# Pinning the order of the gates' products and the pd additions on VectorE, in a spectral filter with a feed-forward block

## Chip, cores and metric

The kernel runs on one core of a Trainium2 chip. The metric is the device time of one execution in microseconds (us); before the change its median is 2563.24 us over 3 runs (2560.34 to 2566.03). TensorE is called PE here, with PEld for its weight loads; VectorE is DVE, ScalarE is ACT, GpSimd is POOL, and SP issues the DMAs.

## What is computed

The input has 8 batches of 3008 rows with 256 columns. The first half filters each batch in the frequency domain; the second is a feed-forward block with a gate:

```python
X = np.fft.rfft(x, axis=1)
Yr = Xr @ w_r - Xi @ w_i + b_r
Yi = Xr @ w_i + Xi @ w_r + b_i
Y  = soft_threshold(Yr, 0.01) + 1j * soft_threshold(Yi, 0.01)
y  = np.fft.irfft(Y, n=3008, axis=1)
h  = y @ w_in
g  = h * np.clip(h + 3.0, 0.0, 6.0) / 6.0
out = g @ w_out
```

w_in has 256 x 2048 elements, w_out 2048 x 256. The change touches the feed-forward block alone, and there the gate, g.

## The kernel before

**Tiles and units.** The 24064 rows are cut into 47 chunks of 512 (T). The 2048 hidden columns are cut into 8 pairs of 128. A unit is one chunk with one such pair, so there are 376 units, numbered i in the order of `units` (line 595). A unit computes h of 2 x 128 hidden columns by 512 rows, its gate, and its share of the chunk's output. Operands of large products are split into a rounded part and the rest (hi and lo), and a product is three matmuls: lo x hi, hi x lo, hi x hi.

**The product with w_in.** It is a Strassen-like scheme with seven blocks of three matmuls (`block`, line 598) in four phases. Phase a (line 612) puts block 2 into PSUM bank pd and block 1 into bank pb; ACT copies pb out as p1 (`kept`, line 602), and DVE adds pd and p1 into the first quarter of h (`added`, line 607). Phase b adds block 6 to pb and copies it out as u2. Phase c adds block 7 to pb, puts block 5 into bank pc, copies pb out as u3, and DVE adds pc and u3 into another quarter of h. Phase d adds block 4 to pb and block 3 to pc; ACT copies pb into h (line 639), and DVE adds pc and u2 into the last quarter. pd and pc have one bank each, pb has two; the transforms' ps_a has two, and the output's po0 and po1 have one each.

**The gate** (`gate`, line 642) is a generator of two steps. The first lets ACT compute r = relu(h + 3) (line 646). The second lets DVE make the product min(r, 6) * h (line 648, a SCALAR_TENSOR_TENSOR over 128 x 1024 elements), and then splits it: ACT casts it to the rounded half of gs (line 131), DVE subtracts that to get the rest (line 132). There are 3 buffers of h, 2 of r and 2 of gs.

**The product with w_out** (`down`, line 660) has 24 matmuls per unit in four steps (line 671). The first 16 read the rounded half of gs, the last 8 the rest.

**The order of the work.** The loop at line 758 traces iteration i in this order: phase a of unit i, second step of the gate of unit i-2, then in turns a quarter of `down` of unit i-3, phase c of unit i-1, phase b of unit i, and phase d of unit i-1 followed by the first step of its gate. After each quarter `fill` (line 746) hands out pieces of other work: the transforms of later batches, the preparation of later chunks and, at the start, the decoding of weights. This traced order is not the order in which the engines run it. The tile framework plans the whole program with a simulated timeline: on each engine it takes, from what is ready in the plan, what was traced first or was marked with `tc.high_priority()`. The additions (line 610) and the copies out of PSUM (line 605) are marked so; the product of the gate is not. On the chip each engine then runs its queue in the order that was planned, and waits on semaphores where operands or buffers are not ready. `tc.issue_after(ins)` adds an edge to the plan: what is traced within it on the engine of `ins` is queued behind `ins`, without a wait for its end.

Of the kernel before, what the change touches and what calls it, by code (L numbers as in the profile page):

```python
# [2 lines left out]

# [1 line left out]

# [10 lines left out]
ALU = mybir.AluOpType  # L16
# [85 lines left out]
def spectral_ffn(ctx: ExitStack, tc: tile.TileContext, x, w_r, w_i, bias, w_in, w_out, f47, f64, g64, sgn, out):  # L102
    nc = tc.nc
# [11 lines left out]
    def space(shape, dt, name, tag=None):  # L115
        tag = tag or name
        return sb.tile(shape, dt, name=name, tag=tag, bufs=depth.get(tag, 1))
# [11 lines left out]
    def split(hi, lo, src, on=None):  # L129

        nc.scalar.copy(out=hi, in_=src)  # L131
        (on or nc.vector).tensor_tensor(out=lo, in0=src, in1=hi.bitcast(F32), op=ALU.subtract)  # L132
# [29 lines left out]
    def loaded(src, rows, cols, name, at=None):  # L162

        hi = const.tile([rows, cols], F32R, name=name + "_hi")
        lo = const.tile([rows, cols], F32R, name=name + "_lo")
        st = const.tile([rows, cols], F32, name=name + "_all") if at is None else at
        nc.sync.dma_start(out=st[:rows, :cols], in_=src)
        return hi, lo, st[:rows, :cols]
# [200 lines left out]
    with tc.issue_after(stores[-1].ins):  # L369
        r, k = [loaded(w, P, 2 * D, n, t) for w, n, t in ((w_r, "w_r", spare[7]), (w_i, "w_i", spare[8]))]  # L370
# [222 lines left out]
            yield  # L593

    units = [(c, f) for c in range(NC) for f in range(nf)]
    hs, ps_of, keep, gs, pos = {}, {}, {}, {}, {}

    def block(i, n, ps, start):
        c, f = units[i]
        product(ps, [(tuple(t[:, f, WEIGHT[n]] for t in win_s), yb[c, n])], start=start, more=True)  # L600

    def kept(i, n, ps):
        t = keep[i, n] = space([P, H], F32, n)
        with tc.high_priority():
            nc.scalar.copy(out=t, in_=ps)  # L605

    def added(i, u, half, ps, n):
        to = hs[i][:, u, half * H : (half + 1) * H]
        with tc.high_priority():
            nc.vector.tensor_tensor(out=to, in0=ps, in1=keep.pop((i, n)), op=ALU.add)  # L610

    def phase_a(i):
        pb = ps_b.tile([P, 512], F32, name="pb")[:, :H]
        pd = ps_c.tile([P, 512], F32, name="pd")[:, :H]
        ps_of[i] = pb
        hs[i] = space([P, 2, T], F32, "h")
        block(i, 2, pd, True)
        block(i, 1, pb, True)
        kept(i, "p1", pb)
        added(i, 0, 0, pd, "p1")  # L620

    def phase_b(i):
        block(i, 6, ps_of[i], False)
# [2 lines left out]
    def phase_c(i):  # L626
        pc = ps_c.tile([P, 512], F32, name="pc")[:, :H]
        block(i, 7, ps_of[i], False)
        block(i, 5, pc, True)
        kept(i, "u3", ps_of[i])  # L630
        added(i, 1, 1, pc, "u3")
        keep[i, "pc"] = pc

    def phase_d(i):
        pb, pc = ps_of.pop(i), keep.pop((i, "pc"))
        block(i, 4, pb, False)
        block(i, 3, pc, False)
        with tc.high_priority():
            nc.scalar.copy(out=hs[i][:, 1, :H], in_=pb)  # L639
        added(i, 0, 1, pc, "u2")  # L640

    def gate(i):

        h = hs.pop(i)
        r = space([P, 2, T], F32, "r")
        nc.scalar.activation(out=r, in_=h, func=AF.Relu, bias=three, scale=1.0)  # L646
        yield
        nc.vector.scalar_tensor_tensor(out=r, in0=r, scalar=6.0, in1=h, op0=ALU.min, op1=ALU.mult)  # L648
        t = gs[i] = space([P, 2, 2, T], F32R, "gs")
        split(t[:, 0], t[:, 1], r)  # L650
        yield
# [105 lines left out]
    n = len(units)  # L757
    for i in range(n + 3):
        for kind, f in ((in_band, i), (out_band, i - 3)):
            while 0 <= f < nf and (kind, f) not in ready:  # L760
                turn(LATE)
        if i < n:
            phase_a(i)
        gated(i - 2)
        fill(4 * i)
        if 0 <= i - 3 < n:
            down(i - 3, 0)
        if 0 <= i - 1 < n:
            phase_c(i - 1)
        fill(4 * i + 1)  # L770
        if 0 <= i - 3 < n:
            down(i - 3, 1)
        if i < n:
            phase_b(i)
        fill(4 * i + 2)
        if 0 <= i - 3 < n:
            down(i - 3, 2)
        if 0 <= i - 1 < n:
            phase_d(i - 1)
            gates[i - 1] = gate(i - 1)  # L780
            gated(i - 1)
        fill(4 * i + 3)
        if 0 <= i - 3 < n:
            down(i - 3, 3)
            gs.pop(i - 3)
# [47 lines left out]
```

## Time and profile before

| what | value |
|---|---|
| median of 3 runs | 2563.24 us (2560.34 to 2566.03) |
| the profiled execution | 2567.17 us |
| its span, first to last instruction | 2565.4 us |
| granted TensorE clock, mean of the span | 0.989 |
| PE busy | 2502.4 us (98%), 20910 matmuls |
| PEld busy | 2442.0 us (95%) |
| DVE busy | 1964.3 us (77%), 3189 instructions |
| ACT busy | 1821.1 us (71%), 3584 instructions |
| POOL busy | 773.4 us (30%) |
| chain that ended last, by engine | PE 88%, DVE 5%, DMA 3%, ACT 3% |

The profiled execution is one run; its own time is 3.9 us above the median, and its span 1.8 us below its time. Busy time is that of an engine's instructions, with overlaps counted once; matmuls are pipelined, so that the duration of one is longer than the distance to the next. A wait in the list of waits is idle time of an engine that ended when another engine, or a DMA, released it. Idle time of an engine that is not the bottleneck costs nothing by itself.

### The profile page before, as it was taken

To read this page: it belongs to the slowest core of one execution; us is meant where nothing else is said; L and a number is where in the kernel's file an instruction comes from. 1 tells how busy PE (TensorE), PEld (TensorE's weight loads), DVE (VectorE), ACT (ScalarE), POOL (GpSimd) and SP (SyncE) were. 2 spreads that over 40 slices of the span, in tenths; PEclk is the share of its full clock that TensorE was granted. 3 is DMA by queue.
4 is the path that set the end of the run, shared out by engine and by line. 5 is a ranking of instruction groups with operands and counts; after the bars stand their busy time and mean duration, and the time that the engine had idled before them with its cause. 6 is when DMAs were issued, how large, how long until landed. Compare 5 with 4: busy or idle time off the path is not lost.

```text
span 2565.4 us, 53388 instructions
## 1 busy us (share of the span) xinstructions
PE 2502.4 (98%) x20910; PEld 2442.0 (95%) x20910; DVE 1964.3 (77%) x3189; ACT 1821.1 (71%) x3584; POOL 773.4 (30%) x738
## 2 busy tenths in 40 slices
PE   5889999999999999999999999999999999999999
PEld 4579999999999999999999999999999999999998
DVE  7778878878787777777777777877777778676766
ACT  5477777777767777777777777767777777776766
POOL 3343342333222332323323333233321221121310
PEclk8889999999999999999999999999999999999999
DMA  8633432332222322323223222222221121110000
GB/s 241 196 112 108 125 103 81 93 91 68 60 71 85 91 68 61 94 72 95 69 71 92 68 79 76 83 77 83 68 78 57 55 66 51 37 33 25 13 18 17
DMA packets 150115, 200.54 MB, mean 78 GB/s; under 512 B 16847, under 2 KB 103943, under 8 KB 149863
## 3 DMA queue, kind: packets, MB, share of 16 engines
q1 hardware_dynamic: 149863, 197.13, 26.4%
q8 instruction: 164, 2.69, 0.4%
q14 instruction: 88, 0.72, 0.1%
HBM read 97.45 MB, written 74.97 MB: 67 GB/s over the span
## 4 chain that ended last, share of the span: by engine, by line
PE 88%; DVE 5%; DMA 3%; ACT 3%; issue 1%; POOL 0%; SPq 0%; ACTq 0%; DVEq 0%; POOLq 0%
PE po L671 38%; PE pb L160 18%; PE pc L160 9%; PE ps_a L140 7%; PE ps_a L160 7%; PE pd L160 5%; PE ps_a L137 3%; ACT r L646 1%; ACT gs L131 1%; DVE r L648 1%; DMA scr<-a 1%; DVE gs L132 1%; DMA zt<-tc 1%; DMA st<-in_w_out 0%; DMA st<-in_w_in 0%
## 5 line engine op out<-in xcount | busy, mean ns | idle before, releaser
L671 PE MATMUL po<-gs,w_out_hi 128*128 128x256 f32 x6016 | 1026.2, 277 | 0.0
L671 PEld LDWEIGHTS po<-gs,w_out_hi 128*128 128x128 f32 x6016 | 840.9, 188 | 1.6
L648 DVE SCALAR_TENSOR_TENSOR r<-r,h 128x1024 f32<-128x1024 f32 x376 | 481.1, 1280 | 273.0 <-ACT r L646 272.0
L671 PE MATMUL po<-gs,w_out_lo 128*128 128x256 f32 x3008 | 597.1, 278 | 3.5 <-ACT gs L131 2.7
L646 ACT ACTIVATE r<-h,three 128x1024 f32<-128x1024 f32 x376 | 434.5, 1155 | 214.9 <-DVE h L610 212.4
L160 PE MATMUL pb<-yb,w_in_hi 128*128 128x256 f32 x3008 | 565.2, 277 | 1.1 <-DVE yb L132 1.1
L132 DVE TENSOR_TENSOR gs<-r,gs 128x1024 fp32r<-128x1024 f32 x376 | 484.4, 1288 | 100.8 <-ACT gs L131 97.1
L131 ACT CAST gs<-r 128x1024 fp32r<-128x1024 f32 x376 | 395.4, 1052 | 107.5 <-DVE r L648 104.1
L671 PEld LDWEIGHTS po<-gs,w_out_lo 128*128 128x128 f32 x3008 | 457.6, 188 | 8.2 <-ACT gs L131 6.8
L160 PEld LDWEIGHTS pb<-yb,w_in_hi 128*128 128x128 f32 x3008 | 456.9, 188 | 4.7 <-DVE yb L132 1.3
L160 PE MATMUL pb<-yb,w_in_lo 128*128 128x256 f32 x1504 | 425.0, 285 | 2.7 <-ACT yb L131 1.7
L132 POOL TENSOR_TENSOR yb<-T,yb 128x256 fp32r<-128x256 f32 x184 | 171.7, 936 | 821.4 <-ACT yb L131 786.1
L610 DVE TENSOR_TENSOR h<-pc,u 128x256 f32<-128x256 f32 x752 | 314.4, 418 | 113.3 <-PE pc L160 100.8
L605 ACT COPY u<-pb 128x256 f32<-128x256 f32 x752 | 279.3, 373 | 86.5 <-PE pb L160 75.0
L160 PE MATMUL pc<-yb,w_in_hi 128*128 128x256 f32 x1504 | 295.0, 277 | 1.1 <-DVE yb L132 1.1
L160 PEld LDWEIGHTS pb<-yb,w_in_lo 128*128 128x128 f32 x1504 | 283.1, 189 | 8.6 <-ACT yb L131 1.9
L160 PEld LDWEIGHTS pc<-yb,w_in_hi 128*128 128x128 f32 x1504 | 228.2, 189 | 2.2 <-DVE yb L132 1.3
L160 PE MATMUL pc<-yb,w_in_lo 128*128 128x256 f32 x752 | 213.3, 284 | 0.7 <-DVE h L610 0.5
L605 ACT COPY p<-pb 128x256 f32<-128x256 f32 x376 | 139.5, 371 | 61.9 <-PE pb L160 59.9
L639 ACT COPY h<-pb 128x256 f32<-128x256 f32 x376 | 141.5, 376 | 48.6 <-PE pb L160 47.4
L610 DVE TENSOR_TENSOR h<-pd,p 128x256 f32<-128x256 f32 x376 | 156.7, 417 | 12.3 <-ACT p L605 11.5
L132 POOL TENSOR_TENSOR xs<-xin,xs 120x512 fp32r<-120x512 f32 (+1 forms) x45 | 58.4, 1297 | 340.9 <-ACT xs L131 320.6
(147 smaller groups left out, 4006.4 us busy)
## 6 DMA issues: line engine op xcount, KB each, us to landing
bt<-scr SPq DMA_DIRECT2D x96, 256.0 KB, 3.0
scr<-pt SPq DMA_DIRECT2D x96, 256.0 KB, 2.4
zt<-tc SPq DMA_DIRECT2D x376, 64.0 KB, 2.0
out<-ot SPq DMA_DIRECT2D x94, 256.0 KB, 2.1
scr<-a SPq DMA_DIRECT2D x96, 240.0 KB, 2.7
qt<-scr SPq DMA_DIRECT2D x96, 240.0 KB, 3.4
xin<-in_x SPq DMA_DIRECT2D x42, 480.0 KB, 4.5
f<-in_f SPq DMA_DIRECT2D x96, 128.0 KB, 2.8
```

The source lines that it names most:

```text
L131: nc.scalar.copy(out=hi, in_=src)
L132: (on or nc.vector).tensor_tensor(out=lo, in0=src, in1=hi.bitcast(F32), op=ALU.subtract)
L137: first = first()
L140: m()
L160: nc.tensor.matmul(**m)
L605: nc.scalar.copy(out=t, in_=ps)
L610: nc.vector.tensor_tensor(out=to, in0=ps, in1=keep.pop((i, n)), op=ALU.add)
L639: nc.scalar.copy(out=hs[i][:, 1, :H], in_=pb)
L646: nc.scalar.activation(out=r, in_=h, func=AF.Relu, bias=three, scale=1.0)
L648: nc.vector.scalar_tensor_tensor(out=r, in0=r, scalar=6.0, in1=h, op0=ALU.min, op1=ALU.mult)
L671: nc.tensor.matmul(out=pos[dh][:, cols], lhsT=w[:, ft * D + dh * P : ft * D + (dh + 1) * P], rhs=g[:, low, u, cols], start=f == 0 and u == ...
```

## The change

The additions into the first quarter of h are kept by unit in `sums`. When the second step of the gate of unit i is traced, the addition of unit i+2 has just been traced, in phase a of the same iteration. The product is now traced within `tc.issue_after` of that addition, so that DVE's queue has it behind the pd addition of unit i+2. The gates of units 374 and 375, for which there is no such addition, are as before. The cast and the subtraction of the gate get no edge of their own.

```diff
-from contextlib import ExitStack
+from contextlib import ExitStack, nullcontext
...
     units = [(c, f) for c in range(NC) for f in range(nf)]
+    sums = {}
...
     def added(i, u, half, ps, n):
         to = hs[i][:, u, half * H : (half + 1) * H]
         with tc.high_priority():
-            nc.vector.tensor_tensor(out=to, in0=ps, in1=keep.pop((i, n)), op=ALU.add)
+            return nc.vector.tensor_tensor(out=to, in0=ps, in1=keep.pop((i, n)), op=ALU.add)
...
         kept(i, "p1", pb)
-        added(i, 0, 0, pd, "p1")
+        sums[i] = added(i, 0, 0, pd, "p1")
...
         yield
-        nc.vector.scalar_tensor_tensor(out=r, in0=r, scalar=6.0, in1=h, op0=ALU.min, op1=ALU.mult)
+        with tc.issue_after(sums[i + 2].ins) if i + 2 in sums else nullcontext():
+            nc.vector.scalar_tensor_tensor(out=r, in0=r, scalar=6.0, in1=h, op0=ALU.min, op1=ALU.mult)
```

## Rows read from the trace of the kernel before

**Rows 1.** Busy us of each engine by stretch (xinstructions), then clock, DMA.
```profile
200.00:2290.00 2090.00, 2083.39 (x17733) 2056.87 (x17733) 1629.05 (x2653) 1515.25 (x2999) 637.87 (x600) 1.00 0.26 76
2290.00:2545.00 255.00, 254.18 (x2203) 252.11 (x2202) 177.60 (x273) 178.79 (x340) 55.03 (x59) 1.00 0.05 18
...
sum 2566.00, PE 2502.36 PEld 2442.04 DVE 1964.30 ACT 1821.10 POOL 773.44; mean PE 625.59 PEld 610.51 DVE 491.07 ACT 455.27 POOL 193.36
```

**Rows 2.** Waits of the whole run: who waited for whom, us, times, longest.
```profile
DVE r L648 <- ACT r L646: 272.0, 291, 2.5
ACT r L646 <- DVE h L610: 212.4, 240, 2.7
```

**Rows 3.** Waits of PE, then of PEld, from 200 us to the end.
```profile
PE po L671 <- ACT gs L131: 2.7, 4, 1.3
...
PE pd L160 <- DVE h L610: 1.0, 2, 0.7
...
PEld po L671 <- ACT gs L131: 6.6, 16, 1.6
PEld pd L160 <- DVE h L610: 2.1, 5, 0.9
...
PEld pc L160 <- DVE h L610: 1.4, 5, 0.5
```

**Rows 4.** DVE's timeline at three places: start, duration, what, idle time before.
```profile
159.33 1.22 DVE L648 SCALAR_TENSOR_TENSOR r<-r,h 128x1024 f32<-128x1024 f32 x1
...
161.93 0.42 DVE L610 TENSOR_TENSOR h<-pd,p 128x256 f32<-128x256 f32 x1
...
1509.44 0.41 DVE L610 TENSOR_TENSOR h<-pd,p 128x256 f32<-128x256 f32 x1
1509.84 1.23 DVE L648 SCALAR_TENSOR_TENSOR r<-r,h 128x1024 f32<-128x1024 f32 x1
...
2546.60 1.23 DVE L648 SCALAR_TENSOR_TENSOR r<-r,h 128x1024 f32<-128x1024 f32 x1 [1.28 <-ACT r L646]
2547.75 0.42 DVE L610 TENSOR_TENSOR h<-pd,p 128x256 f32<-128x256 f32 x1
```

**Rows 5.** Groups of the page: count, busy us, mean ns, idle before, releaser.
```profile
L648 DVE SCALAR_TENSOR_TENSOR r<-r,h 128x1024 f32<-128x1024 f32 x376 | 481.1, 1280 | 273.0 <-ACT r L646 272.0
...
L646 ACT ACTIVATE r<-h,three 128x1024 f32<-128x1024 f32 x376 | 434.5, 1155 | 214.9 <-DVE h L610 212.4
...
L610 DVE TENSOR_TENSOR h<-pd,p 128x256 f32<-128x256 f32 x376 | 156.7, 417 | 12.3 <-ACT p L605 11.5
```

**Rows 6.** Timeline of one unit's gate in the last stretch.
```profile
2332.74 1.23 DVE L648 SCALAR_TENSOR_TENSOR r<-r,h 128x1024 f32<-128x1024 f32 x1 [1.28 <-ACT r L646]
2332.86 0.38 ACT L605 COPY p<-pb 128x256 f32<-128x256 f32 x1
...
2333.99 1.05 ACT L131 CAST gs<-r 128x1024 fp32r<-128x1024 f32 x1 [0.45 <-DVE r L648]
...
2335.11 0.30 PEld L671 LDWEIGHTS po<-gs,w_out_lo 128*128 128x128 f32 x2
```

**Rows 7.** Timeline of one unit's gate in the middle stretch.
```profile
1540.69 1.22 DVE L648 SCALAR_TENSOR_TENSOR r<-r,h 128x1024 f32<-128x1024 f32 x1
1540.80 0.39 ACT L605 COPY p<-pb 128x256 f32<-128x256 f32 x1
...
1541.95 1.05 ACT L131 CAST gs<-r 128x1024 fp32r<-128x1024 f32 x1 [0.45 <-DVE r L648]
...
1544.43 0.30 PEld L671 LDWEIGHTS po<-gs,w_out_lo 128*128 128x128 f32 x2
```

**Rows 8.** Line 648 alone in the last stretch: length, DVE busy (xinstructions).
```profile
2290.00:2545.00 255.00, 59.25 (x48) 1.00 0.05 18
```

**Rows 9.** Sums over five stretches with the addition first, and five with the product first.
```profile
sum 232.00, PE 231.06 PEld 228.81 DVE 185.26 ACT 170.32 POOL 68.65; mean PE 46.21 PEld 45.76 DVE 37.05 ACT 34.06 POOL 13.73
...
sum 754.00, PE 751.36 PEld 742.97 DVE 571.36 ACT 538.77 POOL 223.86; mean PE 150.27 PEld 148.59 DVE 114.27 ACT 107.75 POOL 44.77
```

## The prediction

> **What bounds the kernel now.** I read the busy time of each engine by stretches first, since a share over the whole run averages over stages. In all, TensorE (PE) is busy for 2502.36 us of the 2565.4 us span and VectorE (DVE) for 1964.30 us. Before 200 us the kernel warms up and the gates hardly run; from 200 to 2290 us, where the transforms of later batches run beside the feed-forward units, PE is busy for 2083.39 of 2090 us; from 2290 to 2545 us, where little but the units is left, for 254.18 of 255 us [rows 1]. DVE has room in both: 1629.05 of 2090 us and 177.60 of 255 us. So PE is the bound, and an order on DVE matters only by what it makes PE wait for.
>
> Then the waits. DVE stands idle for 272.0 us before products (line 648) until ScalarE (ACT) has made the relu, and ACT for 212.4 us before relus until DVE has made the additions [rows 2]. Both look large, and both are idle time of engines that are not the bound. What counts is PE's own list, from 200 us on: its weight loads and matmuls wait 6.6 + 2.7 = 9.3 us for a gate's cast (ACT, line 131), 2.1 + 1.0 = 3.1 us for additions before they may write bank pd, and 1.4 us for additions before bank pc [rows 3]. These are 13.8 us, 0.5% of the run, and all that this change can take from PE's waits on gates and additions; PE's work itself is untouched.
>
> **What the change does to the queue.** It adds and removes no operation and no transfer, and neither SP's nor GpSimd's queue is passed. It pins an order: the product of unit i is issued on DVE behind the pd addition of unit i+2. In 101 of the 374 pairs the trace has this order already, as at 1509.44 and 1509.84 us; in 273, from the product at 159.33 us (its addition at 161.93) to that at 2546.60 us (its addition at 2547.75), the product comes first [rows 4]. The last two gates have no such addition and stay free. The edge is one of issue order, so no semaphore is added; but the addition needs its own operand, the p copy of ACT (line 605), so that in practice the product now waits for that too, and the subtraction behind the product, the later additions to h and the other DVE work wait with it. The planner lays out all queues anew around the edge, so PE's and ACT's orders move as well.
>
> **Part 1, the addition that goes ahead.** It was held by at most one product of 1.28 us [rows 5]. PE pays for that only where pd is reused at once: 3.1 us in all [rows 3]. Below nothing it can't go by itself, as an addition issued earlier frees the bank earlier. Bounds: 0 and -3.1 us. I take the share of pairs that change, 273/374 x 3.1 = -2.3 us.
>
> **Part 2, the product that comes later.** Its path is relu, product, cast, and then the first weight load of po, which opens the unit's last product on PE. Two units show both ends. At 2332.74 us the product starts as soon as the relu is there; the p copy ends at 2332.86 + 0.38 = 2333.24, and with 0.42 us for the addition the product could start at 2333.66: 0.92 us late. Now its cast ends at 2333.99 + 1.05 = 2335.04 and PE's load comes at 2335.11, so only 0.07 us of cover stand against it, and 0.85 us would be left on PE [rows 6]. At 1540.69 us the delay is 1540.80 + 0.39 + 0.42 - 1540.69 = 0.92 us again, but the cast ends at 1541.95 + 1.05 = 1543.00 and PE's load comes at 1544.43: 1.43 us of cover, nothing left [rows 7]. The cover is PE's other queued work; without it each of the 273 would cost up to 0.92 us.
>
> Bounds: 0, where the cover holds or the planner, which now knows of the later cast, lays other matmuls in between; and 48 products in the last stretch [rows 8] x 0.85 = +41 us, if each were like the one at 2332.74 and PE's order stayed. I take neither end. What is left of waits in a planned order is where the chip runs later than the plan; the present cast waits of 9.3 us are that. The path grows from 1.155 + 1.28 + 1.05 = 3.49 us to 4.41 us, by 26%; with as many misses per us of path, 9.3 x 0.26 = +2.4 us [rows 3, 5, 6]. This is an estimate.
>
> **Part 3, what comes next.** With the product later, an addition to h from pc that is ready can pass ahead of it or of the subtraction behind the cast, and so the next relu can start earlier: that is the 212.4 us of [rows 2], and against the 0.92 us of delay it is a gain of the same size. I cost it at nothing, between -1.4 us (the waits for bank pc, [rows 3]) and 0.
>
> **The sum:** -2.3 + 2.4 + 0 = +0.1 us. A second reading supports it. The kernel holds both orders in long stretches. In five where all 35 products already follow their addition (581 to 614, 690 to 732, 979 to 1023, 1475 to 1522 and 1961 to 2027 us) PE is busy for 231.06 of 232 us, 99.60%; in five where 116 of 119 precede it (341 to 539, 1529 to 1577, 1602 to 1803, 1830 to 1958 and 2262 to 2441 us) for 751.36 of 754 us, 99.65% [rows 9]. If the difference were due to the order, it would be 0.05% of the 2345 us from 200 to 2545, +1.2 us. The profiled execution took 2567.17 us, 3.9 us over the median of 2563.24; the sum gives 2567.3 us in its terms and 2563.3 us in those of the median. I predict 2563.3 us. About 0.2%, 5.1 us, is what a measurement of this kernel can tell from no change.
>
> **Rivals.** *The additions and gates stop holding PE (faster).* Additions pass early, relus follow earlier, and the regular order brings chip and plan together: all 13.8 us of [rows 3] go, 2549.4 us. For it: the 272.0 and 212.4 us of DVE and ACT waiting for each other [rows 2]. Against: the stretches that have the order show no fewer PE gaps [rows 9]. It counts as faster from 5.1 us on. Chance 0.28.
>
> *The gate's cover runs out in the last stretch (slower).* There PE has few transform matmuls to lay in between, and banks pb, pc and pd are reused each unit. If half of the 48 units kept the 0.85 us, +20 us, 2583.6 us. It decides as soon as 5.1/48 = 0.11 us per unit remain. For it: 0.07 us of cover at 2335 us. Against: PE is at 254.18 of 255 us there [rows 1], so the planner finds work, and the relu may move ahead. Chance 0.20.
>
> *The pinned product blocks its queue (slower).* At 2332.74 us DVE would now idle from the relu's end to the p copy's end, 0.50 us; 273 times that is 137 us of new idle time with subtractions, pc additions and transform work standing behind. If as much of it reached PE as of the present idle time, 13.8/272.0 = 5%, that is +7 us, 2570.2 us. For it: the 272.0 us show that DVE waits at its head while other work stands behind [rows 2]. Against: DVE, busy for 1629.05 of 2090 us [rows 1], can make up for it. Chance 0.10. The Trainium skill, PSUM — Partial Sum Buffer, section Engine vs sequencer instructions, says that VectorE's queue is strictly first in, first out; by that rule nothing behind the product could slip past it, and the 272.0 us agree.
>
> That the change has no effect on the order can't be excluded for the 101 pairs, but the 273 must swap; it would give the time of before and is part of no change.
>
> **How the numbers follow.** No change has 0.42, with its own range of 2558 to 2569 us; faster 0.28; slower 0.20 + 0.10 = 0.30. The range runs from 2550 us, almost the whole of the faster case, to 2581 us, which holds the blocked queue and most of the cover case: about 2 in 10 stay outside.
>
> **What would show it.** In the changed trace every product but the last two follows its pd addition; DVE's idle time before products falls from 272.0 us and comes before pd additions instead, released by the p copy (11.5 us there now in the group of that addition [rows 5]). Part 1 is right if PE's waits for additions at pd nearly vanish, part 2 if its waits for casts stay within 9.3 + 5 us. Casts that hold PE for 20 us or more, above all from 2290 us on, would prove the cover case; a PE share in the middle stretch above 2090 - 1 us busy the faster one.

## The result, and the profile after

The changed kernel takes 2579.04 us (median of 6 runs, 2576.39 to 2581.53) against 2562.52 us before (6 runs, 2560.34 to 2566.18): 16.5 us more, a ratio of 1.0061 with a 95% interval of 1.0051 to 1.0072. It is slower, clearly beyond the 0.2% that count. The time lies in the predicted range, but the likeliest case, no change, did not come true.

The profiled execution of the changed kernel took 2577.22 us, that of the kernel before 2567.17 us. The pair of traces therefore shows 10 of the 16.5 us. Line numbers after are one to two higher: the product is L650, the additions L611, the p copy L606, the last product on PE L673.

Busy time by the same stretches as in [rows 1], after:

```profile
200.00:2290.00 2090.00, 2079.37 (x17618) 2048.76 (x17617) 1606.20 (x2638) 1499.33 (x2982) 664.35 (x598) 1.00 0.27 76
2290.00:2545.00 255.00, 254.91 (x2222) 254.41 (x2221) 181.33 (x275) 183.27 (x343) 58.71 (x60) 1.00 0.05 18
```

In the middle stretch PE has lost 4 us of busy time and, what tells more, done 115 matmuls fewer (17618 against 17733), which have to be done later (in these rows the busy time of PE, PEld, DVE, ACT and POOL follows the length, with the number of instructions in brackets). The last stretch lost nothing: 254.91 us against 254.18. Matmuls are pipelined, so that a short stop shows only in part in PE's busy time.

PE's stops can be added up without that fault from the starts of its matmuls. In the trace before, the next matmul usually starts 113 ns behind one of 256 columns, 231 ns behind one of 512 and 111 ns behind one of 128 or 120; what a distance has over that is a stop. From 200 us on these stops are 44.1 us before and 55.6 us after: 11.5 us more, enough for the 10 us between the two traces. They stand ahead of the matmuls of po that read a fresh cast (`w_out_lo`; 11.1 us before, 17.9 after), of ps_a, the transforms' banks (7.1, 11.0), and of pc (5.6, 8.8); those ahead of pd fell (4.3, 1.3), and the rest changed by 0.5 us in all. So about 7 of the 11.5 us stand where PE takes up a fresh cast.

Waits of PE and then of PEld from 200 us on, after (who waited for whom, us, times, longest):

```profile
PE po L673 <- ACT gs L131: 3.5, 10, 1.0
PE pc L160 <- DVE h L611: 1.8, 5, 0.8
PE ps_a L137 <- DVE raw L565: 1.7, 4, 0.9
...
PEld po L673 <- ACT gs L131: 10.5, 29, 1.2
PEld pc L160 <- DVE h L611: 3.4, 7, 1.0
```

Against [rows 3], waits for casts rose from 9.3 to 14.0 us, those for additions at pc from 1.7 (0.3 of them in PE's list) to 5.2 us; the 3.1 us at pd are gone without a row left. New are waits at ps_a for DVE: 4.4 us in all, 0.2 us before. A stop can stand in both lists, once for the weight load and once for the matmul, so such sums serve to compare kernels and are not additive parts of the span. All of PE's and PEld's waits together rose from 23.8 to 33.5 us.

DVE's own groups, after (count, busy us, mean ns, idle before, releasers):

```profile
L650 DVE SCALAR_TENSOR_TENSOR r<-r,h 128x1024 f32<-128x1024 f32 x376 | 485.3, 1291 | 100.0 <-ACT r L647 99.1
...
L611 DVE TENSOR_TENSOR h<-pd,p 128x256 f32<-128x256 f32 x376 | 157.3, 418 | 129.8 <-ACT p L606 128.7
```

Against [rows 5], the wait has moved: 272.0 us before the product became 99.1 us, and 11.5 us before the pd addition became 128.7 us. DVE waits less at these two places, 227.8 us instead of 283.5, and yet PE loses time. What counts is who stands behind the waiting instruction. One place shows it, in the timeline after:

```profile
531.06 1.17 ACT L647 ACTIVATE r<-h,three 128x1024 f32<-128x1024 f32 x1
...
533.69 0.37 ACT L606 COPY p<-pb 128x256 f32<-128x256 f32 x1 [0.53 <-PE pb L160]
...
534.10 0.42 DVE L611 TENSOR_TENSOR h<-pc,u 128x256 f32<-128x256 f32 x1 [1.81 <-ACT p L606]
534.44 0.41 DVE L611 TENSOR_TENSOR h<-pd,p 128x256 f32<-128x256 f32 x1
...
534.77 1.50 DVE L650 SCALAR_TENSOR_TENSOR r<-r,h 128x1024 f32<-128x1024 f32 x1
...
536.19 0.41 DVE L611 TENSOR_TENSOR h<-pc,u 128x256 f32<-128x256 f32 x1
...
536.66 0.19 PEld L160 LDWEIGHTS pc<-yb,w_in_lo 128*128 128x128 f32 x1 [0.48 <-DVE h L611]
```

The relu of the gate is done at 532.23 us. DVE is idle for 1.81 us until 534.10 and could have made the whole product in that time, but at its head stands an addition from pc, behind that the pd addition, whose p copy ends only at 534.06, and the product is queued behind both. It starts at 534.77, 2.54 us after its relu, and then stands in front of an addition to h from pc, on which PE's next weight load into pc waits for 0.48 us.

In the last stretch the order is the same, but the product is hardly later:

```profile
2331.29 0.37 ACT L606 COPY p<-pb 128x256 f32<-128x256 f32 x1
...
2332.85 0.41 DVE L611 TENSOR_TENSOR h<-pd,p 128x256 f32<-128x256 f32 x1
...
2333.03 1.15 ACT L647 ACTIVATE r<-h,three 128x1024 f32<-128x1024 f32 x1 [0.99 <-DVE h L611]
...
2334.22 1.23 DVE L650 SCALAR_TENSOR_TENSOR r<-r,h 128x1024 f32<-128x1024 f32 x1 [0.95 <-ACT r L647]
```

The addition is over while the relu still runs, and the product starts as soon as the relu is done. Over all units of the last stretch the product starts 0.03 us after the end of its relu before and 0.12 us after it with the pins (means of the two traces); from 200 to 2290 us it is 0.11 us before and 0.75 us after. There the cast ends 0.65 us later behind the relu (3.28 against 2.63 us), and the units whose cast ended less than 0.25 us before PE's first matmul on it rose from 15 of 319 to 47 of 316; in the last stretch they fell from 16 of 47 to 8 of 48.

### The profile page after: what moved, and what is told of

Same layout as the page of the kernel before. It is cut to its first block, busy times and chain, and to the rows that moved or that the text cites. A ratio compares the mean times of both kernels' runs of the same rounds, so it can differ in the third digit from the quotient of the medians.

```text
span 2575.4 us, 53483 instructions
## 1 busy us (share of the span) xinstructions
PE 2509.7 (97%) x20910; PEld 2447.1 (95%) x20910; DVE 1955.1 (76%) x3189; ACT 1818.1 (71%) x3584; POOL 802.9 (31%) x738
## 4 chain that ended last, share of the span: by engine, by line
PE 87%; DVE 5%; ACT 3%; DMA 3%; issue 1%; POOL 1%; SPq 0%; ACTq 0%; POOLq 0%; DVEq 0%
PE po L673 38%; PE pb L160 18%; PE pc L160 9%; PE ps_a L140 7%; PE ps_a L160 7%; PE pd L160 4%; PE ps_a L137 3%; ACT gs L131 1%; DVE r L650 1%; DMA scr<-a 1%; DVE gs L132 1%; DVE h L611 1%; ACT r L647 0%; DMA zt<-tc 0%; DMA xin<-in_x 0%
## 5 line engine op out<-in xcount | busy, mean ns | idle before, releaser
L673 PE MATMUL po<-gs,w_out_hi 128*128 128x256 f32 x6016 | 1019.7, 277 | 0.0
L673 PEld LDWEIGHTS po<-gs,w_out_hi 128*128 128x128 f32 x6016 | 838.4, 188 | 1.2
L673 PE MATMUL po<-gs,w_out_lo 128*128 128x256 f32 x3008 | 600.7, 279 | 4.9 <-ACT gs L131 3.5
L160 PE MATMUL pb<-yb,w_in_hi 128*128 128x256 f32 x3008 | 577.7, 278 | 1.1 <-DVE yb L132 1.1
L132 DVE TENSOR_TENSOR gs<-r,gs 128x1024 fp32r<-128x1024 f32 x376 | 478.2, 1272 | 124.2 <-ACT gs L131 122.6
L650 DVE SCALAR_TENSOR_TENSOR r<-r,h 128x1024 f32<-128x1024 f32 x376 | 485.3, 1291 | 100.0 <-ACT r L647 99.1
L673 PEld LDWEIGHTS po<-gs,w_out_lo 128*128 128x128 f32 x3008 | 457.8, 188 | 13.4 <-ACT gs L131 11.0
L132 POOL TENSOR_TENSOR yb<-T,yb 128x256 fp32r<-128x256 f32 x184 | 200.9, 1096 | 789.7 <-ACT yb L131 718.3
L611 DVE TENSOR_TENSOR h<-pc,u 128x256 f32<-128x256 f32 x752 | 314.8, 419 | 123.4 <-PE pc L160 87.1
L606 ACT COPY u<-pb 128x256 f32<-128x256 f32 x752 | 278.8, 374 | 114.4 <-PE pb L160 100.4
L611 DVE TENSOR_TENSOR h<-pd,p 128x256 f32<-128x256 f32 x376 | 157.3, 418 | 129.8 <-ACT p L606 128.7
L606 ACT COPY p<-pb 128x256 f32<-128x256 f32 x376 | 140.6, 374 | 50.5 <-PE pb L160 49.6
```

The costliest lines, as they stand in the source:

```text
L160: nc.tensor.matmul(**m)
L611: return nc.vector.tensor_tensor(out=to, in0=ps, in1=keep.pop((i, n)), op=ALU.add)
L673: nc.tensor.matmul(out=pos[dh][:, cols], lhsT=w[:, ft * D + dh * P : ft * D + (dh + 1) * P], rhs=g[:, low, u, cols], start=f == 0 and u == ...
```

## The experiments

The kernel before ran beside each of these on the same chip, and ratios are taken to it. Its median was 2564.5 us beside the single pins, the odd units and units 0 to 319, 2564.7 us beside the last units, the opposite order and the swaps, and 2567.8 us beside the copies on DVE and the halves.

**One pin.** The first two were meant to ask how much of the cost is only another plan. The condition is `i == 20`, then `i == 100`:

```diff
-        with tc.issue_after(sums[i + 2].ins) if i + 2 in sums else nullcontext():
+        with tc.issue_after(sums[i + 2].ins) if i == 20 else nullcontext():
```

> Only the product of unit 20 is pinned behind the pd addition of unit 22; all other gates are free. Theory A, the pinned order itself costs time (each pinned product comes later and holds its queue, 16.5 us over 374 pins, 0.044 us per pin): one pin costs nothing, 2562.5 us within 2. Theory B, the planner's new layout: one edge changes the plan of all units after it, and any such plan lands somewhere else, by as much as the full change did: a time 5 to 20 us away from 2562.5 us, on either side.

> Only the product of unit 100 is pinned. Theory A: 2562.5 us within 2, as with unit 20. Theory B: again a time of its own, 3 to 15 us away from 2562.5 us, with no relation to that of unit 20, and somewhat nearer since the first 100 units keep their plan.

Measured: 2568.02 us for unit 20 and 2567.41 us for unit 100, both a ratio of 1.0015 (1.0006 to 1.0023), 3.5 and 2.9 us more. One pin leaves 272 and 273 products ahead of their additions, as before, and waits for casts of 8.9 and 9.6 us. So both theories miss in size: a single pin is not free, but it costs 3 us, not 16. These runs say less of another plan than they were meant to. Compared place by place by the names of their tiles, 457 of PE's 20910 matmuls stand elsewhere than before with unit 20 pinned, all between 307 and 390 us, and 862 with unit 100, all between 850 and 1007 us; then the old order is back. In the changed kernel 15049 stand elsewhere. What a wholly different plan without pins costs is not shown by a single pin.

**Half of the pins, and pins by stretch.** The condition is `i % 2 and i + 2 in sums`, then `i < 320`, and last `i >= 320 and i + 2 in sums`.

> Products of units with an odd number alone are pinned, half of the pins. Theory A: half of the cost, +8 us, 2570 to 2571 us. Theory B: no relation to the number of pins, anywhere from 2550 to 2585 us.

> Pins for units 0 to 319 alone, while the transforms run beside the units; the last 56 gates are free. Theory A: the cost sits there, 2577 to 2580 us, as much as the whole change. The cover rival of the prediction (cost in the last stretch): 2562 to 2565 us. Theory B: no more than 4 us from 2579 us, as the plan up to unit 319 is that of the whole change.

> Pins for units 320 to 373 alone, the last stretch, where the prediction's cover rival put the cost. Cover rival: +15 us or more, 2578 us. Cost in the middle stretch (what the stretches of the changed kernel and the run with pins up to unit 319 point to): no cost here, 2558 to 2565 us, and PE busy from 2290 to 2545 us no less than the 254.2 us of before.

Measured: 2579.88 us with odd units alone, ratio 1.0067 (1.0055 to 1.0080): half of the pins cost as much as all. They turn fewer pairs, 169 instead of 273: 104 products, all of even units, stay ahead of their addition. PE's waits for casts are the highest of these three kernels, 15.8 + 5.9 us:

```profile
PE po L673 <- ACT gs L131: 5.9, 18, 1.0
...
PEld po L673 <- ACT gs L131: 15.8, 41, 1.2
```

Pins up to unit 319 give 2585.52 us, ratio 1.0083 (1.0069 to 1.0097), more than the whole change. Pins from unit 320 on give 2565.46 us, ratio 0.9999 (0.9991 to 1.0008). PE in the last stretch with these alone:

```profile
2290.00:2545.00 255.00, 254.70 (x2202) 253.79 (x2201) 179.76 (x273) 181.11 (x340) 55.87 (x58) 1.00 0.06 18
```

The cost sits in the stretch with transforms beside the units, and the last stretch has none of it. A cost in proportion to the pins is ruled out. Freeing the last 56 gates seems to add some 4 us to the whole change, though the two intervals just overlap. Their order is not the reason: with pins up to unit 319, PE, DVE and ACT have the same order as in the changed kernel up to 2286 us, and yet the matmul at 2233 us runs 8.4 us later in this trace than in that one. Two traces with one order can differ by as much; for the kernel before and the one with the last pins alone it is 2.6 us at the same place. Why stays open, and a difference of a few us between two single traces proves little.

**The opposite order.** The product is put ahead of the addition in all 374 pairs; for this the second step of the gate is traced before phase a.

```diff
+        with tc.issue_after(prods[i - 2].ins) if i - 2 in prods else nullcontext():
+            added(i, 0, 0, pd, "p1")
...
+        prods[i] = nc.vector.scalar_tensor_tensor(out=r, in0=r, scalar=6.0, in1=h, op0=ALU.min, op1=ALU.mult)
```

> The other order pinned: the pd addition of unit i+2 is queued behind the product of unit i, in all 374 pairs (the second step of the gate is traced before phase a for that). Direction theory (the product comes late and PE waits for casts): gates are as early as before or earlier, waits for casts at PE at most 10 us, 2562 to 2568 us. Rigidity theory (any order pinned for all units costs, since an engine that may not take what is ready stands idle): 2575 to 2585 us, with PE waiting for additions at banks pd and pc.

Measured: 2578.46 us, ratio 1.0055 (1.0042 to 1.0067), almost the cost of the change itself. Now it is bank pd that PE waits for:

```profile
PE pd L160 <- DVE h L611: 5.0, 7, 1.1
PE po L673 <- ACT gs L131: 3.6, 5, 0.9
...
PEld po L673 <- ACT gs L131: 8.9, 23, 1.1
PEld pd L160 <- DVE h L611: 8.5, 17, 1.3
```

One place in its timeline:

```profile
1530.67 1.23 DVE L650 SCALAR_TENSOR_TENSOR r<-r,h 128x1024 f32<-128x1024 f32 x1 [1.28 <-ACT r L648]
1531.82 0.42 DVE L611 TENSOR_TENSOR h<-pd,p 128x256 f32<-128x256 f32 x1
...
1532.29 0.19 PEld L160 LDWEIGHTS pd<-yb,w_in_lo 128*128 128x128 f32 x1 [1.18 <-DVE h L611]
```

DVE waits 1.28 us for the relu, makes the product, and only then the addition that PE's load into pd has been waiting for; the addition's p copy was done at 1527.64 us. The mirror image of the place at 534 us: there the product waits behind the addition, here the addition behind the product. The kernel before has pairs in both orders; forcing either on all of them costs about 15 us. By the starts of matmuls, stops ahead of pd rose by 7.5 us (4.3 to 11.8) and those ahead of fresh casts by 3.7 (11.1 to 14.8), of 10.9 us in all. The strict first-in, first-out queue of which the Trainium skill speaks (PSUM — Partial Sum Buffer, Engine vs sequencer instructions) is what both places show, with idle times of 1.81 and 1.28 us at the head and other work behind.

**More cover for the cast.** Phase c of unit i-1 is traced ahead of the first quarter of the w_out product; run without and with the pins.

```diff
-        if 0 <= i - 3 < n:
-            down(i - 3, 0)
         if 0 <= i - 1 < n:
             phase_c(i - 1)
+        if 0 <= i - 3 < n:
+            down(i - 3, 0)
```

> No pins; phase c of unit i-1 is traced before, not behind, the first quarter of the w_out product of unit i-3, which gives the cast six more matmuls (0.7 us) of cover. Control for the next run. Lateness theory: PE's waits for casts fall from 9.3 us to 6 us or less, time 2558 to 2566 us. Rival, phases compete for banks: waits for additions and copies grow, 2565 to 2575 us.

> The whole change with the same swap of phase c and the first quarter. Lateness theory (what the pin costs is the late cast): the extra 0.7 us takes most of the cost, no more than 6 us over the run with the swap alone, casts at PE below 10 us. Queue theory (what the pin costs is DVE's queue held behind the addition): still 10 us or more over the swap alone, and PE's waits for additions at pc and for DVE at ps_a stay near the 5.2 and 4.4 us of the changed kernel.

Measured: 2565.30 us without pins, ratio 1.0007 (0.9998 to 1.0016), with casts at 7.5 us; 2585.78 us with them, ratio 1.0076 (1.0062 to 1.0090), 20.5 us more. With pins:

```profile
PE po L673 <- ACT gs L131: 5.4, 13, 1.3
PE ps_a L160 <- DVE raw L565: 2.8, 1, 2.8
...
PEld po L673 <- ACT gs L131: 12.4, 30, 1.5
PEld pc L160 <- DVE h L611: 3.8, 9, 0.9
```

The swap takes nothing off the cost; the waits at pc (5.3 us) and at ps_a for DVE (8.1 us) stay or grow. But it doesn't test the lateness theory, since the extra cover never reached PE's queue. With the swap alone PE's order differs from that before in 2151 places, all but 85 of them before 700 us, and the mean time from a cast's end to PE's first matmul on it, from 200 to 2290 us, is 1.39 us against 1.42 before. Whether more cover would lower the cost is open.

**The p copy on DVE.** If the cost comes from DVE standing at its head for ACT's p copy, it goes when DVE makes this copy itself.

```diff
-        kept(i, "p1", pb)
+        t = keep[i, "p1"] = space([P, H], F32, "p1")
+        with tc.high_priority():
+            nc.vector.tensor_copy(out=t, in_=pb)
```

> No pins; the p copy out of bank pb runs on DVE instead of ACT, so that the pd addition waits for no other engine but PE. Control for the next run. DVE gets 376 x about 0.42 us = 157 us more work, ACT 141 us less. PE stays the bound: 2562 to 2572 us; rival, DVE at 83% busy makes PE wait for additions: 2575 us or more.

> The whole change with the p copy on DVE. Queue theory (the pin costs because DVE stands at its head for the p copy of ACT, 150 us in the changed kernel, with other work behind): those waits are gone, and the pin costs no more than 6 us over the run with the copy alone. Rigidity theory (any order forced on all units costs, whatever the addition waits for): 10 us or more over it, and PE's waits for casts again above 13 us.

Measured: 2583.85 us without pins (ratio 1.0061, 1.0049 to 1.0074), 2598.86 us with them (1.0118, 1.0105 to 1.0132), 15.0 us more. The copy on DVE alone is as dear as the change: here the rival was right. The pin costs as much as ever although no addition waits for ACT's p copy any more. Without pins 189 products stand ahead of their addition in this kernel, so the pins turn fewer pairs than the 273 of the change. Waits for casts are only 8.8 us this time, so that part of the expectation missed; the stops came elsewhere, in waits for DVE:

```profile
PE ps_a L137 <- DVE raw L565: 3.1, 7, 1.5
PE pc L160 <- DVE h L611: 2.8, 8, 0.7
...
PEld pc L160 <- DVE h L611: 5.3, 12, 0.9
PEld pb L160 <- DVE p L622: 4.4, 13, 0.6
```

**A shorter gate.** Product, cast and subtraction in two halves, without and with pins.

```diff
-        nc.vector.scalar_tensor_tensor(out=r, in0=r, scalar=6.0, in1=h, op0=ALU.min, op1=ALU.mult)
         t = gs[i] = space([P, 2, 2, T], F32R, "gs")
-        split(t[:, 0], t[:, 1], r)
+        for u in range(2):
+            nc.vector.scalar_tensor_tensor(out=r[:, u], in0=r[:, u], scalar=6.0, in1=h[:, u], op0=ALU.min, op1=ALU.mult)
+            split(t[:, 0, u], t[:, 1, u], r[:, u])
```

> No pins; product, cast and subtraction of a gate run in two halves of 512 columns each, so that the first matmuls of po can start after half of the gate and no instruction of the gate holds DVE for more than about 0.7 us. DVE and ACT get 752 and 376 more instructions. Lateness theory: PE's waits for casts (9.3 us) fall to 4 us or less, 2555 to 2562 us. Rival, PE's waits come from where chip and plan differ, and shorter pieces only move them: 2562 to 2572 us.

> The whole change with the gate in halves, both halves of the product pinned behind the pd addition. Lateness theory: the gate is shorter by more than the 0.92 us that the pin delays it, so the pin costs no more than 6 us over the halves alone. Rigidity theory: 10 us or more over the halves alone.

Measured: 2593.15 us without pins (ratio 1.0096, 1.0080 to 1.0111), 2611.64 us with them (1.0170, 1.0156 to 1.0184), 18.5 us more. Both forecasts for the halves alone were too low. PE's waits for casts in the halves alone:

```profile
PE po L672 <- ACT gs L131: 8.4, 20, 1.4
...
PEld po L672 <- ACT gs L131: 14.0, 27, 1.6
```

They rose from 9.3 to 22.4 us. In this kernel only 98 products start ahead of their pd addition without pins, and pinning costs as much all the same. The Trainium skill (Perfetto Trace Analysis, Optimizing Scalar/DVE Operations) says that where these engines aren't saturated but cause bubbles on others, smaller instructions may let work be done sooner. Here DVE was not saturated, and the first half of a cast was done sooner, 1.60 us after the relu in the mean against 2.62 us for the whole cast before. The kernel still took 1% longer: DVE was busy for 2070 instead of 1964 us, and the plan has PE's first matmul on it nearer behind the cast, at 1.04 us in the mean against 1.28; the measurement decides.

None of these kernels is clearly faster than the kernel before.

## Why the prediction was right in its range and wrong in its likeliest case

The time fell into the range because the range reached out to hold two slower rivals; the sum itself, +0.1 us, was wrong by 16.4 us.

**PE as the bound, and the order itself.** Right. The product follows its addition in all 374 pairs of the changed trace. The waits moved from the product to the addition as foretold.

**Part 1, the addition that goes ahead.** Right: the 3.1 us of waits at pd are gone, against the -2.3 us taken and the bound of -3.1 us; by the starts of matmuls it is 3.0 us. (That an addition was held "by at most" 1.28 us misreads a mean; the longest product took 2.32 us.)

**Part 2, the later product.** The path was right, and its price too low. The step said +2.4 us for casts; they rose by 4.7 us in the two lists and by 6.8 us by the starts of matmuls, the largest item of the cost. It failed on where: the late product was read from one unit of the last stretch, 0.92 us late, but with the pins the addition is over before the relu ends in 37 of 48 pairs there, the product starts 0.09 us later behind its relu than before in the mean, and the pins cost nothing. In the middle stretch, where the unit at 1540 us was read as covered, the addition is over in time in only 133 of 316, the product starts 0.64 us later in the mean, and 47 casts instead of 15 end within 0.25 us of PE's first matmul on them. Scaling the old misses by the length of the path can't see that.

**Part 3, what comes next.** This step failed too. It was costed at nothing with bounds from -1.4 to 0 us, on the argument that ready additions would slip past the product. In the changed trace they stand behind it, as at 536.19 us: stops ahead of pc rose by 3.2 us by the starts of matmuls (3.5 us in the lists), and those ahead of ps_a by 3.9 us (4.2 us for DVE in the lists), a place that the working had not listed at all.

**The second reading.** Comparing stretches with one order to stretches with the other was misleading. The planner takes what is ready in its plan, so the stretches with the addition first are probably those in which the addition was ready sooner; that is argued, not shown. They tell nothing of the same order forced where it isn't. The opposite run fits this: it forces the reverse on the 101 pairs that had the addition first, and costs 0.55%.

**The rivals.** The faster one is out. The cover rival came near in its time, 2583.6 us, and casts were the largest item, but in the middle stretch and not in the last, where it put them: its time is luck. The blocked queue was nearest in mechanism: its 137 us of new idle time at the pd addition were measured as 128.7 - 11.5 = 117 us, and its +7 us of PE waits for DVE as 3.5 + 4.2 = 7.7 us. That is a share of 6.6%, where 5% was taken. The rival was too small because casts came on top, and its chance of 0.10 was too low. Its narrow form, that ACT's p copy is what blocks, did not hold.

**What is shown and what is not.** In four kernels (as it was, with the swap, with the copy on DVE, in halves) the pins cost 16.5, 20.5, 15.0 and 18.5 us; the opposite order for all costs 14 us. So pinning this order costs time, and the reverse does too. The starts of matmuls show where: PE stops ahead of fresh casts, ps_a and pc, nearly all in the stretch with transforms beside the units. The places at 534 and 1530 us show how such an order stops PE. In the last stretch the pins hardly delay the product, which starts 0.12 us after its relu there and 0.75 us in the middle stretch; that fits its being spared. One rival is not excluded, that a wholly different plan costs about as much whatever makes it different: the kernels with little or no cost (single pins 3 us, the last pins and the swap none) keep most of PE's order, and those whose order changed throughout all lost 0.5% or more, the copy on DVE and the halves without any pin too. Against it stands that pins cost 15.0 and 18.5 us again on top of those two. How much of the cost is in the plan itself and how much comes from the chip running later than the plan was not separated.

## What to carry to other kernels

On an engine with an in-order queue that serves a bound engine, an idle head is no loss by itself; before pinning an order to remove it, list what will stand behind the pinned instruction and who waits for that. If a scheduler already chooses the order from what is ready, forcing one order everywhere can cost in either direction, and stretches in which it chose that order itself say little about the price. Run the opposite pin as a control; it tells whether the direction matters. Before you read a control, compare the order of the bound engine in both traces: a single pin or a swapped line may be undone by the planner a few units later, and then it says nothing about the rest. Add up the bound engine's stops from the starts of its instructions where these are pipelined; its busy time hides most of a short stop.

## What the runs showed of the hardware that was not expected

The same product of 128 x 1024 elements took very different times beside GpSimd. In the kernel before, 252 products with no GpSimd instruction beside them took 1.228 us at most, and of the 84 with over 0.3 us of one beside them the longest took 2.319 us; in the run with the opposite order one took 4.29 us, with POOL's instructions back to back beside it (timeline of that run):

```profile
657.42 0.74 POOL L587 TENSOR_TENSOR T<-raw,T 128x256 f32<-128x256 f32 x1
...
657.73 4.29 DVE L650 SCALAR_TENSOR_TENSOR r<-r,h 128x1024 f32<-128x1024 f32 x1 [0.66 <-ACT r L648]
...
660.21 0.72 POOL L132 TENSOR_TENSOR yb<-raw,yb 128x256 fp32r<-128x256 f32 x1
...
662.40 0.19 PEld L160 LDWEIGHTS pd<-yb,w_in_lo 128*128 128x128 f32 x1 [1.30 <-DVE h L611]
```

A product stretched so holds all that is pinned behind it, and PE's load into pd waited 1.30 us. That GpSimd is the cause is inferred from what ran beside these products; no run took it away.
